# Loads of v in parts of 24 and 40 partitions, stores of x in parts of 88 and 40

## The chip, the cores and the metric

The kernel runs on one NeuronCore of a Trainium2 chip. Time is device time in microseconds; the kernel before was run three times, with a median of 866.1 us (862.88 to 872.85). One more execution was profiled: it took 868.25 us, with a span of 866.5 us from its first to its last instruction and a mean granted TensorE clock of 0.995. The rows below are of that execution.

## The reference

Talking-heads attention, followed by a bilinear layer, in float32. Sizes: 4 batches, 12 heads, 448 positions, head size 64; the layer is 768 wide with 1536 hidden columns.

```python
scores = scale * np.matmul(q, k.transpose(0, 1, 3, 2))
scores = np.einsum('bhij,hg->bgij', scores, w_pre)        # mix of the heads
scores = scores - np.max(scores, axis=-1, keepdims=True)
attn = np.exp(scores)
attn = attn / (np.sum(attn, axis=-1, keepdims=True) + 1e-09)
attn = np.einsum('bhij,hg->bgij', attn, w_post)           # second mix
attn_out = np.matmul(attn, v)
x = attn_out.transpose(0, 2, 1, 3).reshape(B * S, H * D)
out = (x @ w_a) * (x @ w_b) @ w_out
```

## The kernel before, in words

There are two stages. The **attention stage** fills some 380 us, the **layer** the rest.

Attention goes through 16 chunks of 120 or 88 queries (four to a batch), and each chunk through units of 20 queries; 92 units in all. For a unit, `gather` (line 324) picks the rows of all heads for its queries out of the score tile `s` and puts them on partitions, in four transfers of 60 rows by 448 floats, into the tiles `sb`; POOL issues them, apart from ten in the first five units, which SP issues. Then `premix` (344) multiplies by `w_pre` on TensorE, VectorE takes the maximum (354), ScalarE the exponential (357), `postmix` (390) multiplies by `w_post` and transposes, ScalarE copies the result (407), and `av` (428) multiplies by `v`. The scores of the next chunk (`qk_head`, 280) and their copies (305, 307) run between them. So TensorE's work of one unit is 16 matmuls at 280, 16 at 428, 56 at 390 and 8 at 344.

Six units make a group of `av`. Half of the heads of a group are collected in one PSUM bank, copied to `xs` (437), and stored to the DRAM tile `xd` one step later (438): 32 stores, each of 128 partitions by 3 pieces of 120 (or 88) floats. The layer reads them back (522).

Before the attention stage is through, `load_v` (204) brings each batch's `v`: two head groups of 7 pieces. The pieces numbered 0 to 2 are the first 64 partitions, two heads each (2 KB per partition); 3 and 4 are partitions 64 to 111, three heads each (three runs of 768 B per head group's row); 5 and 6 are small runs of 256 B. Eight pieces of the first batch are issued at the start, ahead of the ten gathers that SP issues. The loads of q and k were already cut by `part` into 88 and 40 partitions (`LOW` is 88).

The order of the work is written out: in each step, `plan_loads` has put loads of q, k and v between `premix` and `norm` by a table of estimated costs. All these loads, the stores of x and two tiny transfers per unit (`pace`, 220), which hold SP back until VectorE has reached the unit, go through SP's one queue. Every transfer that SP issues waits until the eighth one before it has landed (eight semaphores in turn).

Of the kernel before, what the change touches and what calls it, by code (L numbers as in the profile page):

```python
# [22 lines left out]
def talking_heads_bilinear_kernel(  # L23
# [11 lines left out]
    nc = tc.nc  # L35
    B, _, G, S = k.shape
# [10 lines left out]
    R = 4  # L47
    P = S // R
    C = 64
    X = P - C  # L50
# [20 lines left out]
    V_PIECES = 14  # L71
    PACKET = 170
    LOW = 88
    OWN = 3
    SPREAD = 2
    RAW_AT = 74
# [8 lines left out]
    for b in range(B):  # L85
        t0 = 0
        while t0 < S:
            n = min(CHUNK, S - t0)
# [30 lines left out]
    xd = [dram.tile([128, KD, S], F32, name=f"xd{b}") for b in range(B)]  # L119
# [21 lines left out]
    def later(fn, n=3):  # L141
        todo_at.setdefault(now[0] + n, []).append(fn)
# [61 lines left out]
    def load_v(b, i):  # L204
        g, i = divmod(i, V_PIECES // 2)
        to, of = vt[b % 2][g], v[b, g]
        if i < 3:
            heads = slice(2 * i, 2 * i + 2)
            nc.sync.dma_start(out=to[:C, heads], in_=of[:C, heads])
        elif i < 5:  # L210
            heads = slice(3 * (i - 3), 3 * (i - 3) + 3)
            nc.sync.dma_start(out=to[C:P, heads, :R - 1], in_=of[C:, heads, :R - 1])
        elif i == 5:
            for j in range(R - 1):
                nc.sync.dma_start(out=to[P:, :, j], in_=of[C + Y * j:C + Y * j + Y, :, R - 1])
        else:
            nc.sync.dma_start(out=to[C:, :, R - 1], in_=of[:C, :, R - 1])
# [4 lines left out]
    def part(half):  # L222
        return slice(0, 128) if half is None else slice(LOW * half, LOW + (128 - LOW) * half)

# [191 lines left out]
    def av(a, p):  # L416
        b, u0, _ = groups[a]
        t0 = (u0 - b * NUB) * QU
        n = min(AVC, S - t0)
        g = p // 3  # L420
        if p % 3 == 0:
            xp = ps.tile([128, 512], F32, tag="m" if a == NA - 1 else "x", name="xp", bufs=3 if a == NA - 1 else 1)
            xps[g] = xp[:, :3 * AVC].rearrange("p (a t) -> p a t", a=3)
        xp = xps[g]
        for r in range(R):
            for e in range(2):
                h = 2 * p + e
                nc.tensor.matmul(  # L428
                    xp[64 * e:64 * e + 64, p % 3, :n],
                    lhsT=vt[b % 2][g][:, h % G, r],  # L430
                    rhs=ptt[a][:, r, h, :n],
                    start=(r == 0),
                    stop=(r == R - 1),
                )
        if p % 3 == 2:
            xs = x_p.tile([128, 3, AVC], F32, tag="xs", name="xs")
            nc.vector.tensor_copy(xs[:, :, :n], xp[:, :, :n])
            later(lambda: nc.sync.dma_start(out=xd[b][:, 3 * g:3 * g + 3, t0:t0 + n], in_=xs[:, :, :n]), 1)

    items, late, between, after, ready = {}, {}, {}, {}, {}  # L440
    starts = [u for u in range(NU) if units[u][1] == 0] + [NU]
# [2 lines left out]
    for c in range(1, NC):  # L444
        b, t0, _ = chunks[c]
# [11 lines left out]
    for a in range(NA):  # L457
        b, u0, n = groups[a]
        for p in range(H // 2):
            av_at[a, p] = u0 + n + (AV_AT if n == GU else AV_SHORT)[p]  # L460
            if a < NA - 1:
                items.setdefault(av_at[a, p], []).append((av, a, p))

    def plan_loads():
# [6 lines left out]
        def place(first, last, it, n, parts=(0,)):  # L471
            for x in parts:
                u = min(range(min(first, last), last + 1), key=lambda u: (busy[u], u if len(parts) > 1 else -u))
                busy[u] += n
                full = sum(1 for y in between.get(u, ()) if y[0] in (load_q, load_k, load_v))
                (after if full else between).setdefault(u, []).append(it + ((x,) if len(parts) > 1 else ()))
                first = u
# [23 lines left out]
        for b in range(1, B):  # L501
            first = max(av_at[per_b * (b - 2) + per_b - 1, H // 2 - 1] + 1 if b > 1 else 0, V_FIRST + V_PIECES - V_EARLY)
            for i in sorted(range(V_PIECES), key=lambda i: (i // 7, -v_size[i % 7])):
                place(first, av_at[per_b * b, i // 7 * 3] - V_LEAD, (load_v, b, i), v_size[i % 7])
# [346 lines left out]
    with tc.manual_schedule():  # L851
# [16 lines left out]
        for i in range(G):  # L868
            if i == 1:
                spread_q(0, 1, nc.vector)  # L870
                setup_w()
            if i + 4 < G:
                load_k(0, i + 4)
                order_k(0, i + 4, pool, pool)
            if i == 2:
                load_q(1, 0)
                load_q(1, 1)
                for j in range(V_EARLY):
                    load_v(0, j)
            qk(0, i, 0)  # L880
# [17 lines left out]
        for s in range(NU + 2):  # L898
# [19 lines left out]
            for it in items.get(s, ()):  # L918
                if it[0] is qk:
                    it += (it[2] % OWN if s not in late else 1,)  # L920
                it[0](*it[1:])
# [15 lines left out]
        for p in range(6):  # L937
            av(NA - 1, p)
            if p == 2:
                for fn in split_all(2):  # L940
                    fn()
# [73 lines left out]
        for n in range(NP * 2):  # L1015
            i, r = divmod(n, R6)
# [59 lines left out]
```

## Time and profile before

| what | value |
|---|---|
| median of 3 runs | 866.1 us (862.88 to 872.85) |
| the profiled execution | 868.25 us, span 866.5 us |
| TensorE busy | 840.8 us, 97% |
| VectorE / ScalarE / POOL busy | 498.2 / 414.9 / 477.1 us |
| DMA packets | 105246, 165.90 MB, 191 GB/s |
| packets of SP's queue (q1) / of POOL's (q0) | 76998 / 28128 |

In the rows, PE is TensorE's matmul, PEld its weight load, DVE is VectorE, ACT ScalarE, and SP the engine that issues most transfers; a q behind an engine's name is its sequencer. "issue" is time in which an engine waited for nothing that the profile shows. The queue q8 carries instructions. The DMA share is the time that packets took, divided by the length of the stretch and by 16 engines; a share times 16 is the number of engines at work.

### The profile page before, as it was taken

To read this page: it belongs to the slowest core of one execution; us is meant where nothing else is said; L and a number is where in the kernel's file an instruction comes from. 1 tells how busy PE (TensorE), PEld (TensorE's weight loads), DVE (VectorE), ACT (ScalarE), POOL (GpSimd) and SP (SyncE) were. 2 spreads that over 40 slices of the span, in tenths; PEclk is the share of its full clock that TensorE was granted. 3 is DMA by queue.
4 is the path that set the end of the run, shared out by engine and by line. 5 is a ranking of instruction groups with operands and counts; after the bars stand their busy time and mean duration, and the time that the engine had idled before them with its cause. 6 is when DMAs were issued, how large, how long until landed. Compare 5 with 4: busy or idle time off the path is not lost.

```text
span 866.5 us, 26219 instructions
## 1 busy us (share of the span) xinstructions
PE 840.8 (97%) x10612; PEld 674.5 (78%) x10612; DVE 498.2 (57%) x989; ACT 414.9 (48%) x864; POOL 477.1 (55%) x591
## 2 busy tenths in 40 slices
PE   8799999999999989999999999999999999999998
PEld 4355656655656555798999999999999998999997
DVE  5587777867787767455433433354445245655762
ACT  3577767767777768644323322332233145333330
POOL 5776677758757856026447533668666743222220
PEclk9999999999999999999999999999999999999999
DMA  6677697879879975674634644656565497654551
GB/s 189 181 197 182 170 213 202 182 174 209 202 171 205 202 190 124 180 241 151 199 132 149 204 146 134 209 201 239 191 253 189 134 335 292 210 218 187 202 204 65
DMA packets 105246, 165.90 MB, mean 191 GB/s; under 512 B 49794, under 2 KB 81134, under 8 KB 105126
## 3 DMA queue, kind: packets, MB, share of 16 engines
q1 hardware_dynamic: 76998, 126.54, 45.7%
q0 software_dynamic: 28128, 37.68, 18.4%
q8 instruction: 84, 1.38, 0.7%
q14 instruction: 36, 0.29, 0.1%
HBM read 84.16 MB, written 41.29 MB: 145 GB/s over the span
## 4 chain that ended last, share of the span: by engine, by line
PE 85%; DMA 5%; DVE 3%; issue 2%; SPq 2%; POOL 2%; ACT 1%; DVEq 0%; POOLq 0%
PE xp L428 9%; PE pp L390 9%; PE mp L344 7%; PE pst L280 7%; PE pb L640 6%; PE pa L638 6%; PE pa L640 6%; PE pa L639 6%; PE pb L639 6%; PE pb L638 6%; PE po L758 6%; PE po L759 6%; PE po L757 6%; DMA sb<-s 2%; DMA qraw<-in_q_dram 1%
## 5 line engine op out<-in xcount | busy, mean ns | idle before, releaser
L324 POOL DMA_DIRECT2D sb<-s x350 | 202.2, 593 | 53.3 <-PE mp L344 23.5
L357 ACT ACTIVATE a<-mp,nm 124x448 f32<-124x448 f32 x180 | 112.7, 631 | 60.1 <-DVE nm L354 60.1
L354 DVE TENSOR_REDUCE nm<-mp 124x1 f32<-124x448 f32 x180 | 104.1, 619 | 62.0 <-PE mp L344 61.3
L660 DVE TENSOR_TENSOR hf<-pb,sa 128x448 f32<-128x448 f32 x47 | 29.3, 624 | 169.2 <-PE pb L640 149.8
L428 PEld LDWEIGHTS xp<-pt,v 128*64 128x64 f32 x1536 | 73.9, 136 | 62.4 <-issue 44.3
L407 ACT COPY pt<-pp 128x480 f32<-128x480 f32 x176 | 91.3, 576 | 36.3 <-PE pp L390 36.1
L644 ACT COPY sa<-pa 128x448 f32<-128x448 f32 x47 | 25.2, 535 | 173.7 <-PE pa L640 173.7
L390 PE MATMUL pp<-kr,a 60*64 60x60 f32 x5040 | 99.3, 222 | 6.5 <-issue 5.9
L390 PEld LDWEIGHTS pp<-kr,a 60*64 60x64 f32 x5040 | 86.7, 135 | 23.6 <-issue 12.2
L344 PE MATMUL mp<-sb,wp 60*64 60x448 f32 x720 | 97.4, 550 | 6.1 <-DMA sb<-s 5.4
L640 PE MATMUL pb<-xhl,wl 128*128 128x448 f32 x282 | 102.3, 363 | 0.9 <-POOL wl L623 0.9
L639 PE MATMUL pb<-xhl,wh 128*128 128x448 f32 x282 | 102.2, 362 | 0.0
L638 PE MATMUL pb<-xhl,wh 128*128 128x448 f32 x282 | 102.2, 362 | 0.0
L280 PE MATMUL pst<-k,q 64*64 64x448 f32 (+1 forms) x728 | 93.4, 550 | 4.8 <-DVE s L305 2.3
L638 PE MATMUL pa<-xhl,wh 128*128 128x448 f32 x264 | 95.7, 362 | 0.0
L639 PE MATMUL pa<-xhl,wh 128*128 128x448 f32 x264 | 95.7, 362 | 0.0
L640 PE MATMUL pa<-xhl,wl 128*128 128x448 f32 x264 | 95.7, 362 | 0.0
L428 PE MATMUL xp<-pt,v 128*64 128x120 f32 (+1 forms) x1536 | 93.4, 265 | 0.9 <-ACT pt L407 0.8
L629 POOL TENSOR_TENSOR wl<-v,wh 128x768 fp32r<-128x768 f32 x21 | 39.2, 1868 | 98.9 <-ACT wh L628 98.9
L758 PE MATMUL po<-hhl,wh 128*128 128x448 f32 x252 | 91.5, 363 | 1.6 <-DVE hhl L716 1.6
L757 PE MATMUL po<-hhl,wh 128*128 128x448 f32 x252 | 91.3, 362 | 0.0
L759 PE MATMUL po<-hhl,wl 128*128 128x448 f32 x252 | 91.3, 362 | 0.0
(117 smaller groups left out, 1431.0 us busy)
## 6 DMA issues: line engine op xcount, KB each, us to landing
sb<-s POOLq DMA_DIRECT2D x346, 105.0 KB, 5.0
hhl<-hd SPq DMA_DIRECT2D x42, 448.0 KB
v<-in_w_ab_dram SPq DMA_DIRECT2D x22, 768.0 KB
hd<-hf SPq DMA_DIRECT2D x48, 224.0 KB
v<-in_w_out_dram SPq DMA_DIRECT2D x12, 768.0 KB
wod<-cw SPq DMA_DIRECT2D x21, 384.0 KB
v<-wod SPq DMA_DIRECT2D x21, 384.0 KB
xhl<-xd SPq DMA_DIRECT2D x24, 224.0 KB
```

The lines of the kernel that those rows point to most:

```text
L280: nc.tensor.matmul(out[64 * e:64 * e + cols.stop - cols.start], lhsT=qt[c, i // QG][rows, i % QG, cols], rhs=kt[b, i][rows],)
L324: (nc.sync if u <= AH and i % 2 else nc.gpsimd).dma_start(out=sbt[u][i % 2][r:r + m * H], in_=rows)
L344: nc.tensor.matmul(mt[u, i // 2][col:col + M], lhsT=wp[r:r + m, :M], rhs=tiles[i % 2][r:r + m])
L357: nc.scalar.activation(a[:m], mp[:m], ACTF.Exp, bias=nm[:m], scale=1.0, accum_out=rss[u][:m, j:j + 1])
L390: nc.tensor.matmul(pp_t[i][C * e:C * e + C, H * r:H * r + H, j, :m], lhsT=at[u, j][rows, x:x + C], rhs=kr[rows, j, :, :m],)
L428: nc.tensor.matmul(xp[64 * e:64 * e + 64, p % 3, :n], lhsT=vt[b % 2][g][:, h % G, r], rhs=ptt[a][:, r, h, :n], start=(r == 0), stop=(r == ...
L638: nc.tensor.matmul(o, lhsT=hh[:, off + k], rhs=x[:, 0, k], start=first, stop=False)
L639: nc.tensor.matmul(o, lhsT=hh[:, off + k], rhs=x[:, 1, k], start=False, stop=False)
L640: nc.tensor.matmul(o, lhsT=ll[:, off + k], rhs=x[:, 0, k], start=False, stop=last)
L757: nc.tensor.matmul(po, lhsT=hh[:, k], rhs=t[:, 0, k], start=(k == 0), stop=False)
L758: nc.tensor.matmul(po, lhsT=hh[:, k], rhs=t[:, 1, k], start=False, stop=False)
L759: nc.tensor.matmul(po, lhsT=ll[:, k], rhs=t[:, 0, k], start=False, stop=(k == KH2 - 1))
```

## The change

The three pieces of the first 64 partitions of `v` are cut by partition first: 24 partitions with all six heads (6 KB per partition in one run), and 40 partitions twice, three heads each (3 KB). The two pieces of the 48 partitions above are cut into 24 and 24 partitions, six heads each. Each store of x is issued as two, of 88 and of 40 partitions. Nothing is computed otherwise, and the planner's table of costs stays as it was, so each piece of `v` keeps its place.

```diff
+    C_LOW = 24
...
         if i < 3:
-            heads = slice(2 * i, 2 * i + 2)
-            nc.sync.dma_start(out=to[:C, heads], in_=of[:C, heads])
+            rows, heads = ((slice(0, C_LOW), slice(0, G)), (slice(C_LOW, C), slice(0, 3)), (slice(C_LOW, C), slice(3, G)))[i]
+            nc.sync.dma_start(out=to[rows, heads], in_=of[rows, heads])
         elif i < 5:
-            heads = slice(3 * (i - 3), 3 * (i - 3) + 3)
-            nc.sync.dma_start(out=to[C:P, heads, :R - 1], in_=of[C:, heads, :R - 1])
+            n = X // 2
+            rows = slice(C + n * (i - 3), C + n * (i - 3) + n)
+            nc.sync.dma_start(out=to[rows, :, :R - 1], in_=of[rows, :, :R - 1])
...
-            later(lambda: nc.sync.dma_start(out=xd[b][:, 3 * g:3 * g + 3, t0:t0 + n], in_=xs[:, :, :n]), 1)
+            for half in range(2):
+                rows = part(half)
+                later(lambda rows=rows: nc.sync.dma_start(out=xd[b][rows, 3 * g:3 * g + 3, t0:t0 + n], in_=xs[rows, :, :n]), 1)
```

The orders of PE, DVE, ACT and POOL are the same in both kernels. SP's queue changes at two kinds of places. At the start, ahead of the gathers that SP issues (`v_106` and `v_107` are the two head groups of the first batch, `sb` the gathered scores), it was:

```order
L250 DMA qraw<-in_q_dram 128x360 x2
L209 DMA v_106<-in_v_dram 64x512 x3
L212 DMA v_106<-in_v_dram 48x3x192 x2
L215 DMA v_106<-in_v_dram 16x6x64 x3
L217 DMA v_106<-in_v_dram 64x6x64
L209 DMA v_107<-in_v_dram 64x512
L324 DMA sb<-s 60x1x448 x6
```

and now, two lines further down in the code:

```order
L252 DMA qraw<-in_q_dram 128x360 x2
L210 DMA v_106<-in_v_dram 24x1536
L210 DMA v_106<-in_v_dram 40x768 x2
L214 DMA v_106<-in_v_dram 24x6x192 x2
L217 DMA v_106<-in_v_dram 16x6x64 x3
L219 DMA v_106<-in_v_dram 64x6x64
L210 DMA v_107<-in_v_dram 24x1536
L326 DMA sb<-s 60x1x448 x6
```

The number of transfers and their places are the same, only their shapes differ. At the first store of x in the attention stage (`xd_88` is the first batch's x), SP's queue was:

```order
L250 DMA qraw<-in_q_dram 88x360
L250 DMA qraw<-in_q_dram 40x360
L438 DMA xd_88<-xs 128x3x120
L220 DMA paced<-nm 1x1
L234 DMA kraw<-in_k_dram 88x448
```

and now:

```order
L252 DMA qraw<-in_q_dram 88x360
L252 DMA qraw<-in_q_dram 40x360
L442 DMA xd_88<-xs 88x3x120
L442 DMA xd_88<-xs 40x3x120
L222 DMA paced<-nm 1x1
L236 DMA kraw<-in_k_dram 88x448
```

Each of the 32 stores has become two neighbours, so whatever stands behind one has one transfer more ahead of it.

## Rows read from the trace of the kernel before

**Rows 1.** The page, parts 1 and 4: busy time, and the chain by engine.

```profile
PE 840.8 (97%) x10612; PEld 674.5 (78%) x10612; DVE 498.2 (57%) x989; ACT 414.9 (48%) x864; POOL 477.1 (55%) x591
...
PE 85%; DMA 5%; DVE 3%; issue 2%; SPq 2%; POOL 2%; ACT 1%; DVEq 0%; POOLq 0%
```

**Rows 2.** Windows: length, busy time per engine, granted clock, DMA share, GB/s.

```profile
60.00:100.00 40.00, 39.28 (x984) 23.59 (x977) 31.24 (x85) 29.21 (x71) 27.06 (x49) 1.00 0.74 182
...
140.00:180.00 40.00, 39.82 (x996) 24.73 (x992) 32.72 (x87) 29.97 (x74) 26.54 (x48) 1.00 0.74 181
180.00:220.00 40.00, 37.74 (x950) 23.52 (x952) 26.81 (x66) 27.55 (x68) 31.53 (x61) 1.00 0.89 205
...
260.00:300.00 40.00, 38.63 (x976) 24.29 (x976) 29.31 (x70) 29.66 (x73) 32.04 (x59) 1.00 0.96 203
...
400.00:700.00 300.00, 300.00 (x1502) 281.53 (x1500) 125.63 (x135) 89.99 (x127) 179.38 (x108) 1.00 0.54 187
```

**Rows 3.** What PE waited for in 60 to 340 us: total, times, longest.

```profile
PE pp L390 <- issue: 5.9, 7, 1.8
PE pst L280 <- DVE s L305: 1.3, 2, 0.6
```

**Rows 4.** Timeline of PE: start, duration, instructions, idle time before and its releaser.

```profile
188.84 0.51 PE L390 MATMUL pp<-kr,a 60*64 60x60 f32 x19 [1.23 <-issue]
...
210.08 0.63 PE L390 MATMUL pp<-kr,a 60*64 60x60 f32 x29 [1.03 <-issue]
...
293.10 0.50 PE L390 MATMUL pp<-kr,a 60*64 60x60 f32 x18 [1.22 <-issue]
...
305.50 1.00 PE L390 MATMUL pp<-kr,a 60*64 60x60 f32 x28 [1.76 <-issue]
```

**Rows 5.** The page, part 3: instruction queue q8, packets, MB, share of 16 engines.

```profile
q8 instruction: 84, 1.38, 0.7%
```

**Rows 6.** DMA queues in 60 to 340 us: packets, MB, share.

```profile
q0 software_dynamic: 23952, 32.30, 49.4%
q1 hardware_dynamic: 28368, 19.97, 30.4%
q8 instruction: 54, 0.88, 1.4%
```

**Rows 7.** DMA queues in 295.40 to 295.60 us, the packets that start there.

```profile
q8 instruction: 1, 0.02, 57.3%
```

**Rows 8.** DMA queues in 302.60 to 302.80 us.

```profile
q8 instruction: 1, 0.02, 33.6%
```

**Rows 9.** Short windows, the columns as in rows 2.

```profile
21.80:22.30 0.50, 0.50 (x8) 0.00 (x0) 0.50 (x1) 0.00 (x0) 0.00 (x0) 1.00 0.33 125
55.10:55.35 0.25, 0.25 (x10) 0.25 (x8) 0.09 (x1) 0.25 (x2) 0.25 (x1) 1.00 0.70 224
243.20:243.50 0.30, 0.30 (x8) 0.15 (x4) 0.30 (x2) 0.30 (x2) 0.30 (x2) 1.00 0.65 221
255.75:256.00 0.25, 0.25 (x8) 0.25 (x9) 0.25 (x1) 0.24 (x1) 0.00 (x0) 1.00 1.11 313
...
27.03:27.15 0.12, 0.12 (x6) 0.12 (x4) 0.12 (x1) 0.03 (x1) 0.12 (x1) 1.00 0.24 90
305.50:308.90 3.40, 3.40 (x47) 1.94 (x46) 0.74 (x2) 1.05 (x3) 1.95 (x6) 0.51 1.02 172
```

**Rows 10.** Timeline of SP: start and duration of the issue, line, transfer.

```profile
21.95 1.76 SPq L324 DMA_DIRECT2D sb<-s  x2
...
54.25 0.29 SPq L234 DMA_DIRECT2D kraw<-in_k_dram  x1
...
241.86 0.30 SPq L234 DMA_DIRECT2D kraw<-in_k_dram  x1
...
254.56 0.44 SPq L438 DMA_DIRECT2D xd<-xs  x1
```

**Rows 11.** DMA queues in 25.95 to 26.05 us.

```profile
q8 instruction: 1, 0.02, 81.7%
```

**Rows 12.** Chain of waits in 12 to 33 us: start, length, what.

```profile
12.61 1.57 SPq L209
...
14.29 0.96 SPq L324
...
20.86 4.27 DMA qraw<-in_q_dram
...
26.73 5.85 DMA sb<-s
...
32.72 0.98 PE mp L344
```

**Rows 13.** What SP's queue waited for in 60 to 340 us.

```profile
SPq L220 <- DVE rc L368: 54.5, 47, 2.7
SPq L220 <- DVE nm L354: 31.5, 37, 3.5
SPq L220 <- DMA v<-in_v_dram: 5.8, 8, 1.5
```

**Rows 14.** The chain of waits over the whole span, two gathers in it.

```profile
66.36 4.38 DMA sb<-s
...
336.36 3.35 DMA sb<-s
```

## The prediction

> **What bounds the kernel now.** I read the page first. TensorE is busy for 840.8 of 866.5 us, and the chain that ended last runs on it for 85%, on transfers for 5%, in "issue" for 2% [rows 1]. So a change of transfers can act only where TensorE stands still for one. Then the windows: in the layer, 400 to 700 us, TensorE has no gap at all and the DMA share is 0.54; in stretches of 40 us of the attention stage it loses 0.2 to 2.3 us, and the two with a DMA share of 0.89 and 0.96 lose most [rows 2]. The waits of TensorE in 60 to 340 us name what it loses there: 5.9 us before postmix under "issue", and hardly anything else [rows 3]. The timeline shows the four long gaps, of 1.23, 1.03, 1.22 and 1.76 us [rows 4].
>
> "issue" has no releaser in the profile, so I looked for one among the queues. q8 carried 84 packets, 1.38 MB, which is 16.4 KB each [rows 5]; TensorE's 10612 matmuls and 10612 weight loads divided by 84 are 253 instructions per packet [rows 1]. I read q8 as TensorE's instruction stream, a block at a time. In 60 to 340 us there are 54 packets, one in 5.2 us [rows 6], but the packet ahead of the longest gap started at 302.6 to 302.8 us, 7.2 us after the one before it at 295.4 to 295.6 [rows 7, 8]; the gap ended at 305.50. The gaps are blocks of code that come late because their transfer queues behind data.
>
> Then on which engines data and code lie. Alone in 21.80 to 22.30 us are gathers that SP issued: 125 GB/s at a share of 0.33, so five engines, 25 GB/s each [rows 9, 10]. Parts of k's loads, of 88 and 40 partitions, reach 224 and 221 GB/s at shares of 0.70 and 0.65: ten or eleven engines [rows 9, 10]. A store of x, whole, reaches 313 GB/s at 1.11: all sixteen, 19.6 GB/s each, the slower for runs of 480 B [rows 9, 10]. Last, a code packet that started at 25.95 to 26.05 us held its engine for 0.817 x 16 x 0.1 = 1.3 us [rows 11]; inside it, at 27.03 to 27.15 us, the same kind of gathers drop to 90 GB/s at 0.24, four engines for five [rows 9]. So in that place the code came through one of the five engines that SP's short transfers use, and I take it that transfers which spread over fewer engines share those: the parts would load the engine of the code more, and the upper five or six less.
>
> **The change part by part.** *A store of x in two parts.* Whole, an engine carries 128/16 = 8 rows of 1440 B, 11.5 KB, 0.59 us at 19.6 GB/s. In parts, a low engine carries 88/11 = 8 rows and 40/10 = 4 rows, 17.3 KB, 0.88 us: +0.29 us for a store of 120 columns, +0.22 for one of 88. A batch has six and two of them: +2.2 us per low engine.
>
> *v's pieces.* Per head group, the first 64 partitions (6 KB each) took 64/16 x 6144 = 24.6 KB of each engine. Now the two parts of 40 partitions take 2 x 40/10 x 3072 = 24.6 KB. For 24 partitions the trace has no row; between 8 and 16 engines lie 18.4 and 9.2 KB, and I take 12 engines, since the nearest row, 40 partitions, also fills about two thirds: 12.3 KB. The upper 48 partitions took 13.8 KB over sixteen engines and take 18.4 KB over twelve. So +16.9 KB per group, +33.8 KB per batch, 1.35 us at 25 GB/s. The Trainium skill (DMA: Bandwidth & Descriptors, "Why a DMA increments its semaphore by 16 and not by 1") gives the largest number up to 16 that divides the partitions, so 12 for 24, and the lowest-numbered engines; no run here shows 24.
>
> Both together put 3.5 us per batch on each low engine, in some 80 us (a quarter of the 320 us from 60 to 380). **Late code**: the gaps stand in the two stretches of 0.89 and 0.96, or 5 us behind one [rows 2, 4], where added work has no idle time to vanish in. Each is half a batch long and gets 1.75 us. Bounds: 0, if the planner's other transfers leave air around each block, and 2 x 1.75 = 3.5 us; in the calmer stretches, at 0.74, it disappears. The rows show gaps already, so I take a value near the upper end: **+2.5 us**. By the Trainium skill (Runtime: NRT & Kernel Launch, "Instruction fetch mechanics") crossing a block of 16 KB is "mostly hidden", which would make this term nothing and the forecast 867; the 5.9 us of gaps in this trace speak against it.
>
> **The start.** Ahead of SP's gathers stand eight pieces of v, of which six change: four of 64 partitions and two of 48, 46.6 KB per engine, become 67.6 KB on the low ones: +21 KB, 0.84 us. The gathers use five of these engines, and the chain runs from SP's pieces through its gathers to a load of q, POOL's gathers and premix at 32.72 us without slack [rows 12]. Bounds 0 and 0.84; half of the pieces go out while the first loads of q are in flight anyway, so **+0.5 us**.
>
> **Gathers at a batch's or chunk's edge.** Two stand in the chain with 4.38 and 3.35 us [rows 14]. Their slowest engine gets slower by at most the 0.29 us of a store: 0 to 0.6, I take **+0.3 us**.
>
> *SP's time.* 32 issues more, 0.29 us for a part against 0.44 for a whole store [rows 10]: 2 x 0.29 - 0.44 = 0.14 us each, 4.5 us in all, hidden by the 86 us that SP stands waiting for VectorE in the same stretch [rows 13]. If that cover were gone, loads of q and k would come later by the 0.14 us, against a lead of four steps. The pairs also use up the eight semaphores faster: SP waited 5.8 us for v's landings [rows 13], behind it stand the tiny pacing transfers and the next loads, with VectorE's wait as the cover again. The last stores of x are read back by the layer's fourth batch, after three others. All at nothing.
>
> **Sum**: 2.5 + 0.5 + 0.3 = +3.3 us on the profiled 868.25 us, 871.6. That execution stands 2.15 us above the median of the runs, so the forecast is **869.4 us**; about 1% is what a measurement here can tell from no change.
>
> **The rivals.** *Nothing to see (866).* Nobody waits soon for a store or for v, and only packets change places; for it speaks that TensorE loses just 5.9 us in the stage, against it that those 5.9 us stand where transfers are densest. The Trainium skill has a rule that says it too (DMA: Bandwidth & Descriptors, "Rules for kernel authors"): two transfers to disjoint partitions share the same engines, so don't bother; the parts of k on ten or eleven engines [rows 9] differ from it. 20%.
>
> *Slower, by the clock (875.5).* Behind the gap of 1.76 us the granted clock was 0.51 for 3.4 us [rows 4, 9], the lower level of 1.2 GHz, which cost 1.7 us more; behind 1.23 us no window shows a drop [rows 2]. If the three gaps of 1.03 to 1.23 us grow by some 0.6 us to the size of the fourth, each costs 0.6 + 1.7: 6.9 us. With the fourth 0.6 longer, one block more that just misses (1.0) and the 0.8 of start and edges, +9.3: 877.5 by the profiled execution, 875.4 by the median. It decides from about 0.6 us of growth, twice what one store adds to an engine. 18%.
>
> *Faster (858.5).* If the code's engine is not among the low ones in most places (my reading rests on one packet), or the upper engines hold back what matters, then x and v leave them: per batch 8 stores' 11.5 KB and v's 77 KB, some 7.5 us of work. The gaps could close: 5.9 + 1.7 for the clock = 7.6 us, 858.5. Against it speaks the drop from five engines to four. 12%.
>
> **How the numbers follow.** The forecast, 867.5 to 872, has 50%. The predicted time is its 869.4. The range takes in no change with its scatter, the upper bounds of the three terms (3.5 + 0.84 + 0.6 = 4.9, 871) and most of the clock rival: 861 to 877. More than 1% faster is below 857.4: half of the faster case and little else, 7%. More than 1% slower is above 874.8: most of the clock rival and some of the forecast's tail, 18%. Within 1%: 75%.
>
> **What would show it.** In the changed kernel's profile: the line for postmix under "issue" above 5.9 us, longer or more gaps at 180 to 220 and 260 to 310 us, the premix of 32.72 us [rows 12] later by up to 0.8, no change after 400 us, and packets of parts of x at shares near 0.7. The prediction is wrong if the "issue" line falls, or if the time moves while it stays; and the step that would have failed is the place of the code's engine.

## The result, and the profile after

The changed kernel takes 873.84 us (median of 22 runs, 866.79 to 890.22), the kernel before 867.55 us beside it (22 runs, 862.88 to 873.97). The ratio is 1.0058 with a 95% interval of 1.0037 to 1.0079, so +5.0 us (3.2 to 6.9). Two of the 22 runs, 883.21 and 890.22 us, fell into a slower state of the chip, and the ratio, like every comparison below, leaves such runs out. Forecast were +3.3 us and a time of 869.4. The profiled execution took 872.62 us, 4.4 more than that of before, with a span of 870.9 us.

The page of the changed kernel, parts 1 and 4, answers to [rows 1]:

```profile
PE 842.2 (97%) x10612; PEld 677.1 (78%) x10612; DVE 501.0 (58%) x989; ACT 414.6 (48%) x864; POOL 475.9 (55%) x591
...
PE 77%; DMA 9%; DVE 3%; POOL 3%; issue 3%; SPq 2%; ACT 1%; DVEq 0%; POOLq 0%; ACTq 0%
```

TensorE's work is as before; the chain runs more over transfers, 9% in place of 5%. The windows, to be read beside [rows 2], show where:

```profile
140.00:180.00 40.00, 36.72 (x880) 22.50 (x876) 29.08 (x76) 25.89 (x63) 26.76 (x48) 0.96 0.78 190
180.00:220.00 40.00, 40.00 (x985) 24.07 (x978) 30.69 (x71) 29.49 (x73) 29.87 (x57) 1.00 0.78 196
...
260.00:300.00 40.00, 39.72 (x1032) 24.70 (x1032) 31.16 (x74) 30.80 (x77) 30.70 (x54) 1.00 0.81 186
300.00:340.00 40.00, 35.04 (x836) 22.00 (x828) 27.12 (x61) 26.84 (x66) 29.38 (x54) 0.91 0.88 196
...
400.00:700.00 300.00, 299.39 (x1497) 281.11 (x1498) 128.05 (x138) 88.48 (x125) 177.46 (x105) 1.00 0.53 184
```

The layer is unchanged. In the attention stage the two stretches on which the prediction rests, 180 to 220 and 260 to 300, lose 0.0 and 0.3 us now (2.3 and 1.4 before); 140 to 180 and 300 to 340 lose 3.3 and 5.0 (0.2 and 2.5 before). Rows 2 leave out 300 to 340 of the kernel before, which lost more than the two named there, at a DMA share of only 0.75:

```profile
300.00:340.00 40.00, 37.47 (x907) 22.66 (x896) 26.57 (x65) 28.76 (x70) 26.76 (x46) 0.96 0.75 181
```

The waits of TensorE in 60 to 340 us, against [rows 3]:

```profile
PE pp L392 <- issue: 4.4, 6, 1.9
PE pp L392 <- ACT pt L409: 4.4, 1, 4.4
```

"issue" before postmix fell from 5.9 to 4.4 us. New is one wait of 4.4 us for ScalarE. The timeline of TensorE has the two longest gaps, and the windows behind them the clock:

```profile
167.20 1.27 PE L392 MATMUL pp<-kr,a 60*64 60x60 f32 x42 [1.86 <-issue]
...
316.54 2.11 PE L392 MATMUL pp<-kr,a 60*64 60x60 f32 x53 [4.41 <-ACT pt L409]
```

```profile
167.20:171.50 4.30, 4.30 (x65) 2.55 (x66) 1.35 (x3) 1.81 (x5) 2.76 (x6) 0.60 0.73 166
...
316.50:320.00 3.50, 3.46 (x65) 2.65 (x69) 0.62 (x3) 3.39 (x8) 2.19 (x5) 0.50 1.08 237
```

The gaps of [rows 4] are gone from their places; others stand elsewhere, and behind the two longest the granted clock was near its lower level for 3.5 to 4.3 us, twice where it was once.

How the two executions run against each other can be seen from the premix matmuls. These rows have 400, 604, 620, 636 and 716 of them ahead; before, and then changed:

```profile
206.09 0.94 PE L344 MATMUL mp<-sb,wp 60*64 60x448 f32 x8
...
300.54 0.94 PE L344 MATMUL mp<-sb,wp 60*64 60x448 f32 x8
...
311.12 0.94 PE L344 MATMUL mp<-sb,wp 60*64 60x448 f32 x8
...
319.02 0.94 PE L344 MATMUL mp<-sb,wp 60*64 60x448 f32 x8
...
358.06 0.96 PE L344 MATMUL mp<-sb,wp 60*64 60x448 f32 x4
```

```profile
210.61 0.94 PE L346 MATMUL mp<-sb,wp 60*64 60x448 f32 x8
...
302.54 0.94 PE L346 MATMUL mp<-sb,wp 60*64 60x448 f32 x8
...
309.45 0.96 PE L346 MATMUL mp<-sb,wp 60*64 60x448 f32 x8
...
323.21 0.94 PE L346 MATMUL mp<-sb,wp 60*64 60x448 f32 x8
...
362.46 0.96 PE L346 MATMUL mp<-sb,wp 60*64 60x448 f32 x4
```

The changed kernel is 4.5 us behind at the first row and 2.0 at the second. It is 1.7 ahead at the third, since the kernel before has just lost its own longest gap and the slow clock behind it [rows 4, 9], and two units later 4.2 behind. At the last row it is 4.4 behind, and from there to the end both take 508.4 us. So the wait of 4.4 us and the slow clock behind it cost 5.9 us more than the same two units before. That is the largest single loss, but not the whole story: 4.5 us had been lost at 206 us without it.

What this wait is made of can be read from the chain of waits in 296 to 320 us:

```profile
293.29 6.36 DMA xd<-xs
...
299.66 0.47 SPq L210
...
300.23 8.60 DMA v<-in_w_ab_dram
...
308.89 0.23 SPq L222
...
309.21 5.92 DMA v<-in_w_ab_dram
...
315.14 0.03 ACT cvm L559
...
315.93 0.56 ACT pt L409
```

The second part of a store of x, issued at 293.29, took 6.36 us to land. SP's eighth transfer after it, a piece of v, had to wait for that. Behind it came the parts of a raw weight for the layer (tile `v`, from `in_w_ab_dram`); the first took 8.60 us to land and held SP again, by the same rule, until 308.9; so the last part was issued at 309.21, and ScalarE, which had to convert it, stood still for 5.8 us with the copies for TensorE queued behind. In the kernel before that conversion started at 310.12 with no wait. There the three parts of the weight were issued at 293.89, 297.53 and 301.70 us, here at 300.23, 303.35 and 309.21: 5.8 to 7.5 us later, where TensorE was 2.0 us behind.

The timeline of SP shows the same queue earlier, at 100 to 140 us (start and duration of the issue):

```profile
101.76 1.67 SPq L442 DMA_DIRECT2D xd<-xs  x2
...
108.86 3.08 SPq L442 DMA_DIRECT2D xd<-xs  x2
```

These pairs took SP 1.7 and 3.1 us, where I had set 2 x 0.29 us. The row of a pair takes in a wait between its issues: 0.88 us in the first row, none in the second, whose two issues took 1.61 and 1.43 us. By the view of the tile `xd` (duration in ns: least, median, most), before and after:

```profile
L438 SPq DMA_DIRECT2D xd<-xs x30: 378/436/3134, 63.2 to 366.5; - x30
```

```profile
L442 SPq DMA_DIRECT2D xd<-xs x58: 279/444/2308, 63.2 to 362.7; - x58
```

The median issue of a part is as long as that of a whole store. Summed over 60 to 340 us, the issues of x took 18.0 us before and 38.1 us now. And SP's waits in 60 to 340 us, against [rows 13]:

```profile
SPq L222 <- DVE rc L370: 34.1, 34, 2.8
SPq L222 <- DVE nm L356: 18.9, 25, 1.8
SPq L222 <- DMA v<-in_v_dram: 12.2, 13, 2.0
```

SP's slack towards VectorE fell from 86 to 53 us, its waits for landings of v doubled from 5.8 to 12.2. Summed over all rows of that view, SP waited for VectorE 96.4 us before and 63.0 after, for transfers 19.8 and 43.3. These two sums go through the experiments below.

### The profile page after: what moved, and what is told of

Same layout as the page of the kernel before. It is cut to its first block, busy times and chain, and to the rows that moved or that the text cites. A ratio compares the mean times of both kernels' runs of the same rounds, so it can differ in the third digit from the quotient of the medians.

```text
span 870.9 us, 26254 instructions
## 1 busy us (share of the span) xinstructions
PE 842.2 (97%) x10612; PEld 677.1 (78%) x10612; DVE 501.0 (58%) x989; ACT 414.6 (48%) x864; POOL 475.9 (55%) x591
## 4 chain that ended last, share of the span: by engine, by line
PE 77%; DMA 9%; DVE 3%; POOL 3%; issue 3%; SPq 2%; ACT 1%; DVEq 0%; POOLq 0%; ACTq 0%
PE xp L430 7%; PE pp L392 7%; PE pb L644 6%; PE pa L642 6%; PE pa L644 6%; PE pa L643 6%; PE pb L642 6%; PE pb L643 6%; PE po L762 6%; PE po L763 6%; PE po L761 6%; PE mp L346 5%; PE pst L282 5%; POOL sb L326 2%; DMA sb<-s 2%
## 5 line engine op out<-in xcount | busy, mean ns | idle before, releaser
L282 PE MATMUL pst<-k,q 64*64 64x448 f32 (+2 forms) x728 | 94.0, 557 | 4.9 <-DVE s L307 2.3
L633 POOL TENSOR_TENSOR wl<-v,wh 128x768 fp32r<-128x768 f32 x21 | 39.2, 1867 | 98.9 <-ACT wh L632 96.4
```

The lines of the kernel that those rows point to most:

```text
L282: nc.tensor.matmul(out[64 * e:64 * e + cols.stop - cols.start], lhsT=qt[c, i // QG][rows, i % QG, cols], rhs=kt[b, i][rows],)
```

## The experiments

Each kernel was timed over five rounds beside the kernel before. **A** is the theory of the prediction: parts load the engines that carry the code. **B**: the start. **C**: the number of transfers. **D** (formed after the first eight runs): SP's queue falls behind VectorE, since each transfer waits for the eighth before it, and then loads come late. In the table, the second column is from all runs, and the others are from one profiled execution: in 60 to 340 us SP's waits for VectorE and for transfers and TensorE's wait before postmix under "issue", and last where the attention stage ends (the start, in us, of the premix row with 716 ahead).

| kernel | us against before (95%) | SP for VectorE | SP for transfers | "issue" | stage ends |
|---|---|---|---|---|---|
| before | 0 | 96.4 | 19.8 | 5.9 | 358.1 |
| changed | +5.0 (3.2 to 6.9) | 63.0 | 43.3 | 4.4 | 362.5 |
| e1 v only | +3.1 (0.5 to 5.8) | 97.9 | 18.3 | 5.2 | 355.1 |
| e2 x only | +1.1 (-1.3 to 3.6) | 89.1 | 18.4 | 7.5 | 361.3 |
| e3 start undone | +7.7 (4.7 to 10.7) | 69.0 | 44.0 | 7.3 | 368.8 |
| e4 start only | +1.0 (-1.4 to 3.4) | 90.1 | 21.5 | 4.1 | 356.9 |
| e5 all on even parts | +5.1 (2.4 to 7.7) | 58.5 | 31.4 | 2.7 | 366.0 |
| e6 x as 95 and 33 | +10.4 (7.6 to 13.3) | 53.3 | 60.5 | 1.8 | 368.8 |
| e7 q, k even | +0.3 (-2.2 to 2.8) | 87.8 | 24.5 | 4.2 | 351.3 |
| e8 v as 25 and 39 | +5.3 (2.7 to 7.9) | 65.5 | 47.1 | 2.5 | 358.6 |
| e9 x's 40 by POOL | +4.5 (1.9 to 7.1) | 99.8 | 24.9 | 9.6 | 369.2 |
| e10 92 tiny transfers more | +6.3 (4.0 to 8.8) | 43.4 | 51.8 | 4.3 | 363.3 |
| e11 95 and 33 by POOL | +6.9 (4.5 to 9.3) | 129.3 | 18.7 | 4.1 | 365.8 |
| e12 one pacing transfer | +4.3 (1.6 to 7.1) | 101.5 | 18.8 | 2.9 | 357.7 |

One execution need not be like the others. e7, equal to the kernel before by its runs, ends the stage 6.8 us earlier, and e1, slower by its runs, 3.0 us earlier; so the 4.4 us between the two profiled executions above are within the scatter of single executions. From the end of the stage to the last instruction 508 to 510 us pass in all but e9 (514.8) and e8 (518.9). In e8 the layer itself ran slower at the full granted clock, 1453 matmuls in these 300 us and not 1502 [rows 2]:

```profile
400.00:700.00 300.00, 300.00 (x1453) 271.45 (x1452) 123.71 (x134) 87.70 (x122) 171.99 (x103) 1.00 0.52 175
```

**e1, e2: each part alone.** e1 is the changed kernel with the store whole, e2 the kernel before with the store in parts.

```diff
 e1 (in the changed kernel)
-            for half in range(2):
...
+            later(lambda: nc.sync.dma_start(out=xd[b][:, 3 * g:3 * g + 3, t0:t0 + n], in_=xs[:, :, :n]), 1)
 e2 (in the kernel before): the same two the other way round
```

> Only v in the new parts, stores of x whole. Theory A (late code all through the attention stage, in proportion to the microseconds that each part adds to the low engines: x 2.2, v 1.35 per batch, so of some +5 us x has 3.1 and v 1.9): +1.9 us, and the idle time of TensorE before postmix under issue above 5.9 us. Theory B (the start: v's early pieces ahead of SP's gathers make all later work late by about 4 us): +4, the unit of work at 56.45 us before starts some 4 us later, and hardly anything is added after that. Theory C (the 32 additional transfers in SP's queue): 0.

> Only the stores of x in two parts, v as before. Theory A: +3.1 us, with longer issue gaps before postmix. Theory B: 0 to +1, the first store stands at 50 us or later, so nothing moves before it. Theory C: the whole +5, and a load that lands late shows as a new wait (as the 4.4 us on a raw weight at 316 us).

v has +3.1 us, x +1.1: by these middles the reverse of A's weights, though the intervals overlap, and not C's, since x alone has not the whole 5. The sum, 4.2, is the whole effect within its uncertainty, so the times need no interplay. SP's waits show one: 18 us for transfers with either part, 43 with both. "issue" rose in e2, by 1.6 us, and not in e1, the slower by its runs.

**e3, e4: the start.** In e3 the first batch's v is cut as before; in e4 only the first batch's v is cut anew, and x is whole.

```diff
 e3 (in the changed kernel)
-        if i < 3:
+        if b and i < 3:
 e4 (in e1)
-        if i < 3:
+        if not b and i < 3:
```

> The changed kernel with the first batch's v cut as before (batches 1 to 3 and x stay in parts). Theory A: +4.5 us of +5, since only a quarter of v's share is taken back. Theory B: +1 or less, and premix of the first units starts as in the kernel before (32.72 us). Theory C: +5.

> The kernel before with only the first batch's v in the new parts, the other three batches and x as before. Theory A: +0.5 us. Theory B: +4, with TensorE late by that from the first units on. Theory C: 0.

B falls: with the start undone the loss stays, +7.7, and the start alone has +1.0, near A's 0.5. B came from two profiles whose units had been matched one off. Counted out, 32 premix matmuls lie ahead of the row below in every kernel. It is the fifth premix, in the kernel before, the changed one, e2 and e11:

```profile
37.99 0.93 PE L344 MATMUL mp<-sb,wp 60*64 60x448 f32 x8
```

```profile
38.40 0.92 PE L346 MATMUL mp<-sb,wp 60*64 60x448 f32 x8
```

```profile
39.28 0.93 PE L344 MATMUL mp<-sb,wp 60*64 60x448 f32 x8
```

```profile
36.19 0.93 PE L344 MATMUL mp<-sb,wp 60*64 60x448 f32 x8
```

The changed kernel is 0.4 us late there. But e2 and e11 issue up to that point exactly what the kernel before issues, and stand 1.3 us behind it and 1.8 us ahead: the start scatters by more than the change moves it.

**e5, e7, e8: on which engines the parts lie.**

```diff
 e5: parts of x slice(0, 64), slice(64, 128); C_LOW = 32; v's upper 48 as 32 and 16
 e7: LOW = 80 in the kernel before (q, k in 80 and 48)
 e8: C_LOW = 25 in the changed kernel
```

> The changed kernel with other sizes of parts: x 64 and 64, v's first 64 partitions 32 and 32, its upper 48 32 and 16. As many transfers with runs as long as in the changed kernel, only the partitions are divided otherwise. The Trainium skill (DMA: Bandwidth & Descriptors, Why a DMA increments its semaphore by 16 and not by 1) gives sixteen engines for each of these sizes; no run so far shows them. Theory A (the parts of 88, 40 and 24 partitions load some engines more than others, those that carry the code): the loss goes, 0 against the kernel before, and the issue gaps before postmix return to about 5.9 us. Theory C (the number of transfers, or longer runs of v): it stays, +5.

> The kernel before with the parts of q's and k's loads 80 and 48 partitions in place of 88 and 40 (x whole, v as before). By the shares in the short windows a part of 88 or 40 lies on ten or eleven engines; the same rule of the Trainium skill gives sixteen for 80 and 48. Per batch an engine of the low ones loses 4 rows of 1792 B for each of 6 k and 4 rows of 1440 B for each of 8 q: 89 KB, 3.6 us at 25 GB/s, about what the change adds. Theory A: the mirror image of the change, -3 to -5 us, with issue gaps before postmix of 3 us or less. Theory C: 0.

> The changed kernel with v's first 64 partitions cut into 25 and 39 in place of 24 and 40. The same rule gives five engines for 25 and thirteen for 39, so the five lowest carry 30.7 + 18.4 KB of each head group in place of 12.3 + 24.6, with the upper partitions 29.2 KB more than in the kernel before in place of 16.9: 1.7 times. v alone gave +3.1 us (0.5 to 5.8) as 24 and 40. Theory A: 2 us slower than the changed kernel, +7 against the kernel before, and more issue gaps. Theory C: as the changed kernel, +5.

A misses e5 and e7: parts of even sizes cost as much as 88, 40 and 24 (+5.1), and q and k on even parts gain nothing. In e8 v with more on few engines is not seen to cost more (+5.3), but A's +7 lies inside the interval; what speaks against A there is "issue", 2.5 us where more was forecast. e5 isn't a clean test either, since its parts take SP longer to issue (last section), which could cost what the even division saves. So nothing here shows that, at the doses of this change, the division over engines costs, and e7 speaks against it. That e5's parts lie evenly rests on the Trainium skill's rule (DMA: Bandwidth & Descriptors, "Why a DMA increments its semaphore by 16 and not by 1"). This case's trace leaves it open: a stretch in which nearly all packets are those of a store of x shows twelve engines' worth at work (share 0.75), not all sixteen:

```profile
198.60:199.00 0.40, 0.40 (x8) 0.00 (x0) 0.00 (x0) 0.00 (x0) 0.40 (x2) 1.00 0.75 173
```

C held in these three. No version beat the kernel before; e7 equals it.

**e6, e11: a store of x on few engines.** x in parts of 95 and 33 partitions, v as before; in e11 POOL issues all 64 parts.

```diff
 e6 (in e2)
-                rows = part(half)
+                rows = slice(0, 95) if half == 0 else slice(95, 128)
 e11 (in e6)
-                later(lambda rows=rows: nc.sync.dma_start(
+                later(lambda rows=rows: nc.gpsimd.dma_start(
```

> The kernel before with each store of x in parts of 95 and 33 partitions (v as before). With 88 and 40, x alone gave +1.1 us (-1.3 to 3.6). The same rule of the Trainium skill gives five engines for 95 and eleven for 33, so 19 + 3 = 22 rows on the five lowest in place of 8, where 88 and 40 put 12. Theory A: the loss of x alone times 14 / 4 = 3.5, so some +4 us, at most +12, with a store's share in a short window near 0.3. Theory C: as 88 and 40, +1, since the number of transfers is the same.

> The kernel before with x in parts of 95 and 33 partitions, all 64 issued by POOL. Issued by SP these parts cost +10.4 us, and SP waited 60 us for transfers. The load of the engines is the same here, and SP's queue holds 32 transfers fewer than in the kernel before. Theory A: +10. Theory D: 0 to +3, SP's waits for transfers at 20 us or less; what remains is POOL's 64 issues (some 1 us per pair ahead of the gathers) and gathers that land later.

A heavy dose costs: +10.4 us where 88 and 40 had +1.1, within A's 4 to 12 and against C's 1. The store of e6 in such a stretch works on 0.47 x 16 = 7.5 engines on average, between the five and the eleven of the expectation:

```profile
199.75:200.35 0.60, 0.60 (x8) 0.00 (x0) 0.00 (x0) 0.00 (x0) 0.60 (x2) 1.00 0.47 102
```

But the loss doesn't come through the code: "issue" is the least of all, 1.8 us. What grew is SP's wait for transfers, 60.5 us, and VectorE waited 10.9 us for raw k (1.7 before). A store of 120 columns took, from the issue of its first part to the end of its last packet, 4.5 us at the median in the kernel before, 5.0 in e2 and 5.9 in e6. So the engines act here, as far as can be seen, through the time that a store takes to land. In e11, with SP free of x, 6.9 us are left; the intervals overlap, so the 3.5 us between them aren't certain. POOL's own queue may have a share in the 6.9: in e11 TensorE waited 4.5 us for POOL's copies of q, in the kernel before not at all. But e5 and e6, whose stores SP issues, show 2.4 and 2.7 us of this wait. In e11:

```profile
PE pst L280 <- POOL q L269: 3.0, 2, 2.7
...
PE pst L280 <- POOL q L263: 1.5, 2, 0.8
```

**e10: SP's queue alone.** A third transfer of 4 bytes per unit in the kernel before:

```diff
             pace(2 * u, nm)
+            pace(2 * NU + u, nm)
```

> The kernel before (x whole, v as before) with a third transfer of 4 bytes per unit behind the first of the two that pace SP: 92 more issues in SP's queue, some 0.3 us each, 27 us, and no data to speak of on any engine. Theory D, if the number of transfers alone uses up SP's slack (it waits 96 us for VectorE in 60 to 340 us): SP's wait for VectorE falls to some 65 us, its waits for transfers rise above 30, +2 to +6 us. Theory D, if it takes transfers that land late: 0 to +1, since these land soon. Theory A: 0.

+6.3 us, beyond what A allows, with the same picture as in the changed kernel. The waits of SP and the one of ScalarE, and the chain up to it:

```profile
SPq L220 <- DVE rc L369: 19.0, 22, 1.6
SPq L220 <- DMA v<-in_v_dram: 14.5, 13, 2.5
SPq L220 <- DVE nm L354: 14.4, 20, 2.2
```

```profile
ACT cvm L556 <- DMA v<-in_w_ab_dram: 5.6, 1, 5.6
```

```profile
288.56 5.70 DMA xd<-xs
...
296.96 5.50 DMA v<-in_v_dram
...
302.53 6.42 DMA v<-in_w_ab_dram
...
309.59 5.39 DMA v<-in_w_ab_dram
```

No data to speak of was added and no part was cut, and yet SP lost half of its slack, waited 52 us for landings, and the raw weight came late at the same place. The premix rows with 620 and 636 ahead:

```profile
309.86 0.94 PE L344 MATMUL mp<-sb,wp 60*64 60x448 f32 x8
...
324.00 0.94 PE L344 MATMUL mp<-sb,wp 60*64 60x448 f32 x8
```

1.3 us ahead of the kernel before, and then 5.0 behind: 6.2 us more than there in these two units. As in the changed kernel, that isn't all: with 604 ahead it was 2.4 us behind already (302.96 us). So transfers in SP's queue are enough to produce a loss of this size. ScalarE's wait for the raw weight stands also in the profiles of e5 (6.3 us), e6 (5.3) and e8 (4.3), and is missing or under 2.4 us in those of the kernel before, e1, e2, e4 and e7. Read down the table's third column: of the kernels in which SP issues all the stores and both pacing transfers, those with 87 us or more of waiting for VectorE lose 0 to 3.1 us, and those with 69 or less lose 5.0 to 10.4. In the last column the two groups end at 351 to 361 us and at 359 to 369. e3 is the exception to the place: SP is as short of time there, but the raw weight isn't waited for, and TensorE waits in other places, 3.1 us for VectorE's copies of scores, 1.7 for an ordering of k, 1.4 for a copy of q.

**e9, e12: SP relieved.** In e9 POOL issues the 40-partition parts, in e12 the first pacing transfer is left out.

```diff
 e9 (in the changed kernel)
-                later(lambda rows=rows: nc.sync.dma_start(
+                later(lambda rows=rows: (nc.gpsimd if rows.start else nc.sync).dma_start(
 e12 (in the changed kernel)
-        if j == 0:
-            pace(2 * u, nm)
```

> The changed kernel with the 40-partition part of each store of x issued by POOL in place of SP. Partitions, engines and data are as in the changed kernel; SP issues 32 stores again. Theory D (SP's queue: its waits for transfers that it issued eight places earlier, 20 us in 60 to 340 us in the kernel before, 43 in the changed one, make it fall behind VectorE, and then loads of k, q and raw weights come late): SP's waits for transfers fall to 30 us or less, the loss to 0 to +3 us. Theory A (the engines): +5 as in the changed kernel. A price of its own: 32 issues more on POOL, some 0.6 us each, behind which gathers stand; by this the time could rise by up to 2 us.

> The changed kernel without the first of the two pacing transfers of each unit (the one that waits for the maximum): 92 transfers fewer in SP's queue, and SP is held only at the unit's end, so loads start up to half a unit earlier. Theory D: SP's waits for transfers fall below 30 us, TensorE no longer stands before a raw weight's conversion (4.4 us at 316 us), 0 to +2 us against the kernel before. Theory A: +5, or more as loads bunch.

Both did to SP what D says, in the one execution that was profiled: waits for transfers at 24.9 and 18.8 us, slack at 99.8 and 101.5, and the wait for the raw weight is gone (0.5 us in e12). By their runs neither brought the time back: +4.5 and +4.3. But the two profiles don't show what those runs lose. That of e12 took 868.13 us, the third fastest of its twelve runs, and its stage ends 0.3 us earlier than that of the kernel before, so in this execution the time is back with the relief. The other nine took 873.35 us or more, and none of them was profiled. That of e9 is the slowest of its runs, 885.64 us: SP is relieved there, the stage still ends 11.1 us later, and TensorE's "issue" is 9.6 us. So either these edits cost by themselves what they save (POOL's issues stand ahead of gathers, loads that are held only once per unit bunch), or SP is not relieved in most executions, or SP's queue is one way to lose these 5 us and not the only one. The controls, the same two edits in the kernel before, weren't run; this stays open.

## Why the prediction was right or wrong

- **What bounds the kernel**: right in that all that moved lies before 400 us, with 508.4 us behind the attention stage in both kernels. Wrong was that the two stretches with the densest transfers lose most: 300 to 340 us lost 2.5 us at a share of 0.75.
- **Late code, +2.5 us**: failed, and by its own test: the time moved while "issue" did not rise (5.9 to 4.4). Which engine carries the code, to which the prediction pointed for this case, isn't seen to matter: the time followed the engines neither with the changed parts spread evenly (e5) nor with q and k spread evenly (e7). The gaps of the kernel before are real, but the added 1.75 us per stretch didn't lengthen them in sum; they stand elsewhere. I took four gaps of one profile for a property of the stretch, which they aren't: 180 to 220 us, with two of the four, has none now. By the Trainium skill's "mostly hidden" (Runtime: NRT & Kernel Launch, "Instruction fetch mechanics") the term would have been nothing, and that came out better than my 2.5, although the gap of 1.86 us at 167 us shows that it isn't always so: a packet of q8 started at 164.8 us, 0.5 us before that gap.
- **The start, +0.5 us**: e4 measured +1.0 (-1.4 to 3.4) and the pair of profiles 0.4, in agreement, though neither tells it from nothing.
- **Gathers, +0.3 us**: the median landing of POOL's gathers in 60 to 340 us went from 5.0 to 5.4 us, where at most 0.29 more had been set. Two gathers were counted, but the chain of the kernel before holds a third at 237.34 us, with 4.22 us. What they cost wasn't tried apart.
- **SP's time, "all at nothing"**: this is the step that failed the other way. I priced the issue at 0.14 us per store, 4.5 us in all, by the shortest rows, 0.29 for a part and 0.44 for a store [rows 10]. The medians are 0.444 and 0.436, so the second part costs a full issue; with the long ones the issues of x took 20 us more. And I named the eight semaphores and then set VectorE's 86 us as a cover over the whole stage. That sum is not where the cover is needed: behind a transfer that takes 6.36 us to land, SP stands still, and what it issues next is late whatever slack it had elsewhere. e10 shows that more transfers in SP's queue can cost 6 us with nothing else changed. In the profiled pair the one late weight is the largest single loss, 5.9 us. That it makes the 5.0 us over all runs isn't shown: e3 is slow without it, and e9 and e12, whose profiles lack it, are slow by their runs. So what the 5.0 us are made of stays open in part.
- **Size and sign**: +3.3 forecast, +5.0 measured, 873.8 in the range of 861 to 877, and 0.58%, within 1%. The sum came near with its largest term wrong and another one, set to nothing, in its place: a near hit for a reason that didn't hold.
- **The rivals**: "nothing to see" is excluded by the interval. The rule that two transfers to disjoint partition halves aren't worth it (DMA: Bandwidth & Descriptors, "Rules for kernel authors", in the Trainium skill) agrees in so far as cutting gained nothing; x, the only transfer that was cut in two, cost 1.1 us alone (-1.3 to 3.6). The clock rival's mechanism was there in part: two stretches near the lower level in place of one [rows 9], 3.5 x 0.5 and 4.3 x 0.4, some 1.7 us each, but the one at 316 us stood behind ScalarE's wait, not behind code. Nor does a long gap always bring the lower clock: e2 has gaps under "issue" of 2.1 and 2.5 us, and its granted clock is 1.00 in every 40 us from 60 to 340. "Faster" had no support: no run was clear of the kernel before on that side.

## What to carry to other kernels

Cover for an issuing queue is local: look, at each place where a transfer was added, for how long the one eight places earlier takes to land and for what stands behind, and not at the queue's total of idle time. A transfer that is cut in two costs its queue a second full issue and a second place among the transfers in flight, even where no byte is added. A profile is of one execution: hold a difference between two profiles against the scatter between executions before it is given a cause. And before an offset between two profiles is explained, count the instructions that lie ahead of it in each, and look at the same stretch in kernels that are equal up to there.

## What was unexpected

An issue's duration depends on how the partitions are divided, and not as their number does. In e5 a part of 64 partitions took SP no less than 0.575 us, in the kernel before a whole store of 128 as little as 0.378, both with 3 runs per partition. For e5:

```profile
L441 SPq DMA_DIRECT2D xd<-xs x58: 575/646/3955, 63.2 to 366.6; - x58
```

Nothing here tells why; it may be part of why even parts gained nothing.
